# A gated mix of a state-space layer and a feed-forward layer: first loads in another order, six GELUs ahead of the sines, and part of the angle tables on GpSimd and ScalarE

## The chip, the core and the metric

The kernel runs on one core of a Trainium2 chip. The metric is the device time of one execution in microseconds; the median of 12 runs of the kernel before is 217.12 us. The core has TensorE (matmuls, into PSUM), VectorE, ScalarE, GpSimd, and SyncE, which here only issues transfers. Each engine works through its own instructions in order and waits for the others by semaphores.

## The reference

```python
x = A_x                                            # (1, 2048, 640), bfloat16
g = sigmoid((x * gate_w).sum(-1, keepdims=True))
a = S5(x)      # Bu = x @ B_bar.T ; h_t = Lam_bar * h_(t-1) + Bu_t ; a = 2 * Re(h @ C.T) + x * Dskip
b = gelu(x @ w1 + b1) @ w2 + b2                    # 640 -> 1728 -> 640
return g * a + (1 - g) * b
```

S5 has 640 complex states. `Lam_bar = exp(dt * Lambda)` has a modulus r and an angle theta per state. B_x is not used.

## The kernel before, in words

The 2048 tokens are four chunks of 512. For each chunk there are three matmul stages. `ff1(c)` computes the hidden layer of the feed-forward branch in 13 full tiles of 128 features and a last one of 64 that also holds the gate's column; each tile is five matmuls of 512 columns into one PSUM bank, and one GELU on ScalarE (`ff1_act`, L256) empties the bank into `gel`. `ssm(c)` computes x times B in ten banks, which ScalarE copies to `bu` (L537). `fin_b(c)` and `fin_a(c)` multiply by w2 and by C, and VectorE mixes both into `ot`, which SyncE stores. PSUM has eight banks (pool `ps`).

VectorE runs the recurrence. It turns `bu` by the angle (multiplications with the tables TCOS and TSIN of cosines and sines for 512 steps, L473 and L477), runs a real scan with factor r (L488), and turns the result back into `hs`. `fold(ks)` (L448 to L461) multiplies C by a complex factor: ScalarE fills two `ft` buffers (L451, L453), VectorE combines them (L457).

The tables are made at the start. From the logarithm of dt and the two parts of Lambda, three rows each of five blocks of 128 (`prmA`), a small matmul turns the rows to columns (L327), copied as `colA`. VectorE forms the angles of 128 steps for five blocks (L368 to L370), ScalarE takes sine and cosine (L377, L379) and those of 20 single angles (L385, L386); VectorE extends them to 256 steps (L406 to L411) and to 512 steps block by block (L414 to L421): two casts into the lower half of TCOS and TSIN, and for the upper half a multiplication by a column followed by a multiply-add. A second row tile, `prmB`, holds the bias b1 and the gate's weights (L389, `colB`); the GELUs need it. ScalarE keeps one set of function tables at a time: the exponential, the sine and the GELU each need a table load.

While the weights arrive, TensorE works on chunk 0 by strips. Four strips of 128 tokens are loaded (`load_xn`), turned by matmuls with the identity (`turn`), copied to `xT` by VectorE and ScalarE (`turned`, L223 and L225), and multiplied with those blocks of w1's first 768 columns (`w1a`, five blocks of 128 rows) that are there (`strip`). Six banks collect the first six feature tiles (FA = 6). Blocks 0 and 2 come by ScalarE's queue and serve the strips; blocks 1, then 4 and 3 come by SyncE's queue and serve all 512 tokens at once. Eight matmuls of ones (L213) run before the first strip is there.

TensorE, VectorE and ScalarE run in the order in which the kernel's text issues their instructions. For VectorE this order comes from a planner: `later` puts an operation with a ready time and a cost in a list, and `let_out` issues those that a clock (`ck.dve`, `ck.pe`, `ck.act`) says would have begun. `ck.dve` is set by hand to 27.0 ahead of the first scan (L422). Transfers and GpSimd's instructions are put in order by the framework's scheduler. Each transfer by SyncE's or ScalarE's queue gets one of eight counters in turn, and waits for the last transfer that used the same counter.

Of the kernel before, what the change touches and what calls it, by code (L numbers as in the profile page):

```python
# [10 lines left out]
ALU = mybir.AluOpType  # L11
ACT = mybir.ActivationFunctionType
BF16 = mybir.dt.bfloat16
# [3 lines left out]
P = 128  # L17
# [15 lines left out]
FA = 6  # L33
# [8 lines left out]
def kernel(  # L42
# [38 lines left out]
    xT = [const.tile([P, KD, CH], BF16, name=f"xT{c}") for c in range(NCH)]  # L81
    w1a = [const.tile([P, cut1], BF16, name=f"w1a_{kd}") for kd in range(KD)]
    w1b = [const.tile([P, n1b], BF16, name=f"w1b_{kd}") for kd in range(KD)]
# [31 lines left out]
    def load_xn(c, a0=0, a1=TPC, queue=None):  # L115
        if a0 == 0:
            xn[c] = xnp.tile([P, TPC, D], BF16, name="xn")
        r0 = c * CH + a0 * P
        (queue or nc.sync).dma_start(out=xn[c][:, a0:a1, :], in_=x2d[r0:r0 + (a1 - a0) * P, :].rearrange("(a p) d -> p a d", p=P))

    def load_w1a(queue, kd):
        queue.dma_start(out=w1a[kd][:], in_=B_w1[kd * P:(kd + 1) * P, 0:cut1])

    def rows(queue, dst, v):
        queue.dma_start(out=dst, in_=v.rearrange("(j p) -> j p", p=P))  # L125
# [3 lines left out]
    load_xn(0, 1, 2)  # L129
    load_w1a(nc.scalar, 2)  # L130
    load_xn(0, 2, 3)
    nc.vector.memset(prmA[:], 0.0)
    nc.vector.memset(prmB[:], 0.0)
    rows(nc.scalar, prmA[0:KS, :], A_log_dt)
    rows(nc.scalar, prmA[KS:2 * KS, :], A_Lambda_im)
    rows(nc.scalar, prmA[2 * KS:3 * KS, :], A_Lambda_re)
    load_xn(0, 3, 4)
    for kd in (1, 4, 3):
        load_w1a(nc.sync, kd)
    rows(nc.sync, prmB[KS:NB, :], B_b1[0:(KF - 1) * P])  # L140
# [17 lines left out]
    nc.sync.dma_start_transpose(out=CT_im[:], in_=A_C_im[:, :])  # L158
    nc.sync.dma_start(out=w2_sb[:, 0:KF - 1, :], in_=B_w2[0:(KF - 1) * P, :].rearrange("(kf p) d -> p kf d", p=P))
    for h in range(2):  # L160
# [4 lines left out]
    nc.sync.dma_start_transpose(out=xT[3][:], in_=x2d[3 * CH:4 * CH, :])  # L165
    load_xn(1)

    ctx.enter_context(tc.manual_schedule(engines={E.PE, E.DVE, E.Activation}))

# [38 lines left out]
    ones = lambda n: nc.const_aps.tensor(1.0, [P, n], BF16)  # L208
    warm = const.tile([P, 1], F32, name="warm")
    nc.scalar.activation(out=warm[:], in_=ones(1), func=ACT.Exp)  # L210
    pA = bank()
# [36 lines left out]
    gbs = [None] * NT  # L248
    def ff1_mm(p, c, kf, kd, t0=0, t1=CH, first=None, last=KD - 1):
        w = w1a[kd][:, kf * P:(kf + 1) * P] if kf < FA else w1b[kd][:, (kf - FA) * P:(kf - FA + 1) * P]  # L250
        nc.tensor.matmul(p[:, t0:t1], lhsT=w, rhs=xT[c][:, kd, t0:t1],  # L251
                         start=(kd == 0) if first is None else first, stop=(kd == last), skip_group_check=first is not None)
        pe(t1 - t0)
# [55 lines left out]
    def strip(kd, t0, t1, first, f0=0, f1=FA):  # L309
        for kf in range(f0, f1):  # L310
            ff1_mm(banks[kf], 0, kf, kd, t0, t1, first, 3)

    def turn_all(a):
        tB = bank()
        for i in range(3):
            turn(tB, i * P, a, i)
        turned(nc.vector, tB, 0, a, 0, 1)
        turned(nc.vector, tB, P, a, 1, 3)
        for i in range(2):
            turn(pA, i * P, a, 3 + i)  # L320
        turned(nc.scalar, pA, 0, a, 3, 5)

    strip(0, 0, P, True)
    turn_all(1)
    strip(2, 0, P, False)
    strip(0, P, HT, True)
    nc.tensor.matmul(pA[:, HT:HT + 3 * KS], lhsT=prmA[:], rhs=ident[:, 0:3 * KS], start=True, stop=True, skip_group_check=True)  # L327
    nc.vector.tensor_copy(out=colA[:], in_=pA[:, HT:HT + 3 * KS])
    nc.scalar.activation(out=dt16[:], in_=ldt_c, func=ACT.Exp)
    strip(2, P, HT, False, 0, 3)  # L330
    turn_all(2)
    nc.vector.tensor_copy(out=dt32[:], in_=dt16[:])
    nc.vector.tensor_tensor(out=dtl[:], in0=dt32[:], in1=lre_c, op=ALU.mult)
    nc.vector.tensor_tensor(out=th_c[:], in0=dt32[:], in1=lim_c, op=ALU.mult)
    nc.vector.tensor_scalar(out=thp_c[:], in0=th_c[:], scalar1=INV_2PI, scalar2=None, op0=ALU.mult)
    strip(2, P, HT, False, 3, FA)
    strip(0, HT, HT + P, True)
    turn_all(3)
    nc.scalar.activation(out=r_c[:], in_=dtl[:], func=ACT.Exp)
    strip(2, HT, HT + P, False)  # L340
    strip(0, HT + P, CH, True)
    strip(2, HT + P, CH, False)
    strip(1, 0, CH, False)

# [31 lines left out]

    nc.scalar.activation(out=FS[:, :, 0:HC], in_=red, func=ACT.Sin, scale=TWO_PI_M)  # L377
    nc.vector.scalar_tensor_tensor(out=ab, in0=red, scalar=-1.0, in1=red, op0=ALU.mult, op1=ALU.max)
    nc.scalar.activation(out=FC[:, :, 0:HC], in_=ab, func=ACT.Sin, scale=-TWO_PI_M, bias=halfpi[:])  # L379
    nc.vector.tensor_tensor(out=two[:].rearrange("p (n k) -> p n k", n=NQ), in0=thp_c[:].rearrange("p (o k) -> p o k", o=1).to_broadcast([P, NQ, KS]),  # L380
                            in1=span4[:].rearrange("p (n o) -> p n o", o=1).to_broadcast([P, NQ, KS]), op=ALU.mult)
    nc.vector.tensor_copy(out=kq[:], in_=two[:])
    nc.vector.tensor_tensor(out=redq[:], in0=two[:], in1=kq[:], op=ALU.subtract)
    nc.vector.scalar_tensor_tensor(out=absq[:], in0=redq[:], scalar=-1.0, in1=redq[:], op0=ALU.mult, op1=ALU.max)
    nc.scalar.activation(out=sq[:], in_=redq[:], func=ACT.Sin, scale=TWO_PI_M)  # L385
    nc.scalar.activation(out=cq[:], in_=absq[:], func=ACT.Sin, scale=-TWO_PI_M, bias=halfpi[:])  # L386
    for kf in range(FA):
        if kf == 3:
            nc.tensor.matmul(pA[:, 0:NB], lhsT=prmB[:], rhs=ident[:, 0:NB], start=True, stop=True, skip_group_check=True)  # L389
            nc.vector.tensor_copy(out=colB[:], in_=pA[:, 0:NB])  # L390
            for j in range(KD):
                nc.vector.tensor_copy(out=w1b[j][:, n1b - 1:n1b], in_=pA[:, j:j + 1])
        for kd in (4, 3):
            ff1_mm(banks[kf], 0, kf, kd, 0, CH, False, 3)
    for kf in range(FA):
        ff1_act(banks[kf], 0, kf)
    two_banks = [bank(), bank()]
# [16 lines left out]
    for ks in range(KS):  # L414
        nc.vector.tensor_copy(out=TCOS[:, ks, 0:HB], in_=FC[:, ks, :])
        nc.vector.tensor_copy(out=TSIN[:, ks, 0:HB], in_=FS[:, ks, :])
        for dst, X, xs, Y in ((TCOS, FS, nsH, FC), (TSIN, FC, sH, FS)):
            t = work.tile([P, HB], F32, name="g")
            nc.vector.tensor_scalar(out=t[:], in0=X[:, ks, :], scalar1=xs[:, ks:ks + 1], scalar2=None, op0=ALU.mult)
            nc.vector.scalar_tensor_tensor(out=dst[:, ks, HB:CH], in0=Y[:, ks, :],  # L420
                                           scalar=cH[:, ks:ks + 1], in1=t[:], op0=ALU.mult, op1=ALU.add)  # L421
    ck.dve = 27.0  # L422

# [256 lines left out]
    fin_a(0)  # L680
    load_xn(2)
    ssm(2, {KS - 1: lambda: first_banks(1)})
    fin_b(1, seeds(1))
    fin_a(1)
    load_xn(3)
    ssm(3)
# [38 lines left out]
```

## Time and profile before

| what | us |
|---|---|
| median of 12 runs | 217.12 (216.9 to 218.6) |
| the profiled execution's own time | 216.95 |
| its span, first to last instruction | 215.2 |
| TensorE busy | 209.4 (97%) |
| VectorE busy | 190.1 (88%) |
| ScalarE busy | 101.1 (47%) |
| GpSimd busy | 1.1, in the first 2 us |
| mean granted clock of TensorE | 0.997 |

Times inside the profile count from the span's start. A row of the timeline gives start, duration, engine, line, operation, output and input, and in brackets how long the engine stood idle before it and for whom. The start of an instruction can lie before the end of the one ahead of it, since engines overlap them; the distance of two starts is then what an instruction costs. Busy time by stage:

```profile
core 0: us, PE busy (x) PEld busy (x) DVE busy (x) ACT busy (x) POOL busy (x), PEclk, DMA share, GB/s
...
3.60:5.75 2.15, 1.85 (x16) 1.51 (x15) 0.90 (x4) 1.76 (x3) 0.00 (x0) 1.00 0.92 291
5.75:13.10 7.35, 7.29 (x73) 4.95 (x74) 6.20 (x26) 4.70 (x11) 0.00 (x0) 1.00 1.11 253
13.10:21.50 8.40, 8.35 (x57) 4.22 (x57) 8.16 (x19) 8.39 (x14) 0.00 (x0) 1.00 0.99 196
21.50:57.80 36.30, 36.14 (x186) 16.76 (x186) 35.40 (x88) 22.69 (x40) 0.00 (x0) 1.00 0.86 191
57.80:87.30 29.50, 29.18 (x196) 15.26 (x197) 28.53 (x50) 21.98 (x38) 0.00 (x0) 1.00 0.01 1
```

The columns are the stretch, its length, the busy time and number of instructions of TensorE, of its weight loads, of VectorE, ScalarE and GpSimd, then clock, share and rate of the transfers.

### The profile page before, as it was taken

How to read it: one execution, taken by the hardware profiler on the slowest of the kernel's cores; microseconds unless marked ns; L12 is line 12 of the kernel's file. 1: busy time of each engine (PE TensorE's matmuls, PEld its weight loads, DVE VectorE, ACT ScalarE, POOL GpSimd, SP SyncE). 2: the span in 40 equal slices, each digit the busy share in tenths (PEclk: the TensorE clock that was granted, in tenths of full speed). 3: DMA queues.
4: the chain of work that ended last, by engine and by line, in shares of the span. 5: the costliest groups of instructions: out<-in, count | busy, mean ns of one | idle time of the engine just before them, and what ended most of it. 6: DMA issues, size and time to landing. Idle time of an engine off the chain costs nothing.

```text
span 215.2 us, 3529 instructions
## 1 busy us (share of the span) xinstructions
PE 209.4 (97%) x1366; PEld 117.0 (54%) x1385; DVE 190.1 (88%) x396; ACT 101.1 (47%) x183; POOL 1.1 (0%) x12
## 2 busy tenths in 40 slices
PE   8999999999999999999999999999999999999993
PEld 4745444454454544775445677444455477654773
DVE  2899999999999999898999999799999999994252
ACT  2599556665866696203563210456682422204200
POOL 1000000000000000000000000000000000000000
PEclk9999999999999999999999999999999999999998
DMA  6999999994000000061000005100000000100011
GB/s 203 284 176 205 194 221 339 212 190 132 3 0 0 3 2 0 12 182 64 0 0 3 0 0 186 61 0 2 0 5 12 0 3 30 61 34 0 0 64 62
DMA packets 30324, 15.84 MB, mean 74 GB/s; under 512 B 22883, under 2 KB 30307, under 8 KB 30307
## 3 DMA queue, kind: packets, MB, share of 16 engines
q1 hardware_dynamic: 29844, 15.18, 29.0%
q10 hardware_dynamic: 462, 0.43, 0.6%
q8 instruction: 11, 0.18, 0.3%
q14 instruction: 7, 0.05, 0.1%
HBM read 7.48 MB, written 2.62 MB: 47 GB/s over the span
## 4 chain that ended last, share of the span: by engine, by line
PE 95%; DMA 1%; ACT 1%; issue 1%; DVE 0%; ACTq 0%
PE bank L592 26%; PE bank L251 26%; PE bank L651 20%; PE bank L534 20%; DMA xn<-in_A_x_dram 1%; PE bank L608 1%; PE bank L277 1%; ACT L210 1%; PE bank L216 0%; DVE ot L656 0%; ACT xT L225 0%; ACTq L125 0%; ACT warm L210 0%; PE bank L267 0%; PE bank L389 0%
## 5 line engine op out<-in xcount | busy, mean ns | idle before, releaser
L592 PE MATMUL bank<-w_sb,gel 128*128 128x128 bf16 (+1 forms) x408 | 56.9, 297 | 0.7 <-issue 0.5
L592 PEld LDWEIGHTS <-gel 128*128 128x128 bf16 x416 | 32.2, 98 | 25.5
L537 ACT ACTIVATE bu<-bank 128x512 bf16<-128x512 f32 x40 | 23.9, 597 | 38.9 <-PE bank L534 38.3
L256 ACT ACTIVATE gel<-bank,colB 128x512 bf16<-128x512 f32 x52 | 34.0, 695 | 11.9 <-PE bank L251 11.1
L651 PEld LDWEIGHTS <-hs 128*128 128x128 bf16 x330 | 31.6, 98 | 11.6
L488 DVE TENSOR_TENSOR_SCAN g<-r_c,carry,v 128x512 bf16<-128x512 f32 x30 | 37.4, 1270 | 0.0
L251 PE MATMUL bank<-xT,w1b 128*128 128x512 bf16 x137 | 30.8, 379 | 0.2
L600 ACT ACTIVATE gb<-bank,gcol 128x512 f32<-128x512 f32 (+1 forms) x32 | 15.1, 526 | 33.5 <-PE bank L608 17.3
L251 PE MATMUL bank<-xT,w1a 128*128 128x512 bf16 (+1 forms) x152 | 27.5, 332 | 0.2
L651 PE MATMUL bank<-CT_re,hs 128*128 128x320 bf16 (+2 forms) x165 | 27.1, 295 | 0.0
L651 PE MATMUL bank<-CT_im,hs 128*128 128x320 bf16 (+2 forms) x165 | 27.1, 295 | 0.0
L656 DVE SCALAR_TENSOR_TENSOR ot<-bank,gcol,gb 128x320 bf16<-128x320 f32 (+2 forms) x33 | 17.5, 532 | 10.7 <-PE bank L651 8.7
L534 PE MATMUL bank<-xT,BT_im 128*128 128x512 bf16 x99 | 24.8, 379 | 0.1
L534 PE MATMUL bank<-xT,BT_re 128*128 128x512 bf16 x97 | 24.4, 379 | 0.2
L251 PEld LDWEIGHTS <-w1b 128*128 128x128 bf16 x140 | 13.7, 98 | 16.4
L251 PEld LDWEIGHTS <-w1a 128*128 128x128 bf16 x156 | 13.6, 99 | 12.4
L567 DVE TENSOR_TENSOR bank<-xn,Dbc 128x320 f32<-128x320 bf16 (+2 forms) x33 | 14.5, 480 | 2.0 <-ACT gb L600 1.9
L534 PEld LDWEIGHTS <-BT_im 128*128 128x128 bf16 x100 | 9.8, 98 | 11.8
L469 DVE TENSOR_TENSOR v<-wa,wb 128x512 bf16<-128x512 bf16 x40 | 15.2, 421 | 0.6
L534 PEld LDWEIGHTS <-BT_re 128*128 128x128 bf16 x100 | 9.6, 98 | 11.0
L581 ACT ACTIVATE bank<-b2bc 128x512 f32<-128x512 bf16 (+1 forms) x24 | 11.7, 529 | 7.7 <-DVE ot L656 7.7
L469 DVE TENSOR_TENSOR wa<-TCOS,g 128x1024 bf16<-128x1024 bf16 x20 | 13.7, 685 | 0.1
(100 smaller groups left out, 151.5 us busy)
## 6 DMA issues: line engine op xcount, KB each, us to landing
out_dram<-ot SPq DMA_DIRECT2D x15, 160.0 KB, 1.8
w_sb<-in_B_w_dram SPq DMA_DIRECT2D x1, 2080.0 KB, 10.3
xn<-in_A_x_dram SPq DMA_DIRECT2D x3, 640.0 KB, 5.3
w1b<-in_B_w_dram SPq DMA_DIRECT2D x5, 240.0 KB, 4.3
xn<-in_A_x_dram SPq DMA_DIRECT2D x4, 160.0 KB, 3.3
w1a<-in_B_w_dram SPq DMA_DIRECT2D x3, 192.0 KB, 2.9
w1a<-in_B_w_dram ACTq DMA_DIRECT2D x2, 192.0 KB, 3.3
w2l<-in_B_w_dram SPq DMA_DIRECT2D x2, 80.0 KB
```

The lines of the kernel that those rows point to most:

```text
L251: nc.tensor.matmul(p[:, t0:t1], lhsT=w, rhs=xT[c][:, kd, t0:t1], start=(kd == 0) if first is None else first, stop=(kd == last), skip_grou ...
L256: nc.scalar.activation(out=gel[c][:, kf, :], in_=p[:, :], func=ACT.Gelu_apprx_tanh, bias=b1_c[:, kf:kf + 1])
L469: nc.vector.tensor_tensor(out=o, in0=a, in1=b, op=op)
L488: nc.vector.tensor_tensor_scan(s["g"][:, ri, :], r_c[:, ks:ks + 1].to_broadcast([P, CH]), s["v"][:, ri, :], init, ALU.mult, ALU.add)
L534: nc.tensor.matmul(p[:], lhsT=BT[ks >= KSA][:, kd, (ks % KSA if ks < KSA else ks - KSA) * P:][:, 0:P], rhs=xT[c][:, kd, :], start=(kd == 0 ...
L537: nc.scalar.activation(out=bu[:, ri, :], in_=p[:], func=ACT.Identity)
L567: dve_now(ck.pe, 0.45, lambda: nc.vector.tensor_tensor(out=p[:, 0:d1 - d0], in0=xn[c][:, a, d0:d1], in1=Dbc[:, d0:d1], op=ALU.mult))
L581: nc.scalar.activation(out=v, in_=src, func=ACT.Identity)
L592: nc.tensor.matmul(p[:, col:col + d1 - d0], lhsT=gel[c][:, kf, a * P:(a + 1) * P], rhs=w2_sb[:, kf, d0:d1], start=False, stop=False, skip_ ...
L600: nc.scalar.activation(out=gbs[ti][:, d0:d1], in_=p[:, col:col + d1 - d0], func=ACT.Identity, scale=gcol[:, 1, ti:ti + 1])
L651: nc.tensor.matmul(p[:, 0:d1 - d0], lhsT=hs[c][:, j, lo:lo + P], rhs=CT[:, j % KS, d0:d1], start=False, stop=(j == 2 * KS - 1), skip_group ...
L656: nc.vector.scalar_tensor_tensor(out=ot[:, d0:d1], in0=p[:, 0:d1 - d0], scalar=gcol[:, 0, ti:ti + 1], in1=gbs[ti][:, d0:d1], op0=ALU.mult, ...
```

## The change

- Loads: ScalarE's queue carries w1a's blocks 0 and 1, and blocks 2 and 3 in one transfer of 384 KB (`w1a23`), then loads its first table and runs the small activation that calls for it (`warm`). The three `prmA` rows go to SyncE's queue, behind the four strips; block 4 follows them.
- w2 comes in five transfers instead of one; the token rows of chunks 1 to 3 in two each.
- The strips use blocks 0 and 1; then come block 2 for all tokens, the bias matmul (`prmB`), and blocks 3 and 4. The small matmul for `prmA` moves behind all turns.
- VectorE's copy of `colB` and the five gate columns stand ahead of its work on the angles. The six GELUs of the first tiles stand ahead of the sines.
- Tables to 512 steps: for block 0 VectorE multiplies, for blocks 1 to 4 GpSimd does; the ten casts become two ScalarE copies of 1280 columns. GpSimd now also runs in the text's order from there on, and the products lie in the scratch tile `scr`. `ck.dve` is set to 26.0, and VectorE's planned order changes with it in places up to the end.

```diff
-    load_w1a(nc.scalar, 2)
+    load_w1a(nc.scalar, 1)
     load_xn(0, 2, 3)
+    nc.scalar.dma_start(out=w1a23[:], in_=B_w1[2 * P:4 * P, 0:cut1].rearrange("(k p) f -> p k f", p=P))
+    warm = const.tile([P, 1], F32, name="warm")
+    nc.scalar.activation(out=warm[:], in_=nc.const_aps.tensor(1.0, [P, 1], BF16), func=ACT.Exp)
+    load_xn(0, 3, 4)
     nc.vector.memset(prmA[:], 0.0)
     nc.vector.memset(prmB[:], 0.0)
-    rows(nc.scalar, prmA[0:KS, :], A_log_dt)
-    rows(nc.scalar, prmA[KS:2 * KS, :], A_Lambda_im)
-    rows(nc.scalar, prmA[2 * KS:3 * KS, :], A_Lambda_re)
-    load_xn(0, 3, 4)
-    for kd in (1, 4, 3):
-        load_w1a(nc.sync, kd)
+    rows(nc.sync, prmA[0:KS, :], A_log_dt)
+    rows(nc.sync, prmA[KS:2 * KS, :], A_Lambda_im)
+    rows(nc.sync, prmA[2 * KS:3 * KS, :], A_Lambda_re)
+    load_w1a(nc.sync, 4)
...
-    nc.sync.dma_start(out=w2_sb[:, 0:KF - 1, :], in_=B_w2[0:(KF - 1) * P, :].rearrange("(kf p) d -> p kf d", p=P))
+    for k0, k1 in ((0, 3), (3, 6), (6, 9), (9, 11), (11, KF - 1)):
+        nc.sync.dma_start(out=w2_sb[:, k0:k1, :], in_=B_w2[k0 * P:k1 * P, :].rearrange("(kf p) d -> p kf d", p=P))
...
-    load_xn(1)
-    ctx.enter_context(tc.manual_schedule(engines={E.PE, E.DVE, E.Activation}))
+    for a in (0, H):
+        load_xn(1, a, a + H)
+    ctx.enter_context(tc.manual_schedule(engines={E.PE, E.DVE, E.Activation, E.Pool}))
...
     strip(0, 0, P, True)
     turn_all(1)
-    strip(2, 0, P, False)
+    strip(1, 0, P, False)
     strip(0, P, HT, True)
+    strip(1, P, HT, False, 0, 3)
+    turn_all(2)
+    strip(1, P, HT, False, 3, FA)
+    strip(0, HT, HT + P, True)
+    turn_all(3)
+    strip(1, HT, HT + P, False)
     nc.tensor.matmul(pA[:, HT:HT + 3 * KS], lhsT=prmA[:], rhs=ident[:, 0:3 * KS], start=True, stop=True, skip_group_check=True)
...
     strip(0, HT + P, CH, True)
-    strip(2, HT + P, CH, False)
-    strip(1, 0, CH, False)
+    strip(1, HT + P, CH, False)
+    strip(2, 0, CH, False)
+    nc.tensor.matmul(pA[:, 0:NB], lhsT=prmB[:], rhs=ident[:, 0:NB], start=True, stop=True, skip_group_check=True)
+    nc.vector.tensor_copy(out=colB[:], in_=pA[:, 0:NB])
...
-    nc.scalar.activation(out=FS[:, :, 0:HC], in_=red, func=ACT.Sin, scale=TWO_PI_M)
...
+    for kf in range(FA):
+        for kd in (3, 4):
+            ff1_mm(banks[kf], 0, kf, kd, 0, CH, False)
+    for kf in range(FA):
+        ff1_act(banks[kf], 0, kf)
+    nc.scalar.activation(out=FS[:, :, 0:HC], in_=red, func=ACT.Sin, scale=TWO_PI_M)
+    nc.scalar.activation(out=FC[:, :, 0:HC], in_=ab, func=ACT.Sin, scale=-TWO_PI_M, bias=halfpi[:])
...
     for ks in range(KS):
-        nc.vector.tensor_copy(out=TCOS[:, ks, 0:HB], in_=FC[:, ks, :])
-        nc.vector.tensor_copy(out=TSIN[:, ks, 0:HB], in_=FS[:, ks, :])
-        for dst, X, xs, Y in ((TCOS, FS, nsH, FC), (TSIN, FC, sH, FS)):
-            t = work.tile([P, HB], F32, name="g")
-            nc.vector.tensor_scalar(out=t[:], in0=X[:, ks, :], scalar1=xs[:, ks:ks + 1], scalar2=None, op0=ALU.mult)
+        part = [scr[:, (2 * ks + i) * HB:(2 * ks + i + 1) * HB] for i in range(2)]
+        engine = nc.vector if ks == 0 else nc.gpsimd
+        for t, X, xs in ((part[0], FS, nsH), (part[1], FC, sH)):
+            engine.tensor_scalar(out=t, in0=X[:, ks, :], scalar1=xs[:, ks:ks + 1], scalar2=None, op0=ALU.mult)
+        for dst, t, Y in ((TCOS, part[0], FC), (TSIN, part[1], FS)):
             nc.vector.scalar_tensor_tensor(out=dst[:, ks, HB:CH], in0=Y[:, ks, :],
-                                           scalar=cH[:, ks:ks + 1], in1=t[:], op0=ALU.mult, op1=ALU.add)
-    ck.dve = 27.0
+                                           scalar=cH[:, ks:ks + 1], in1=t, op0=ALU.mult, op1=ALU.add)
+    nc.scalar.activation(out=TCOS[:, :, 0:HB], in_=FC, func=ACT.Identity)
+    nc.scalar.activation(out=TSIN[:, :, 0:HB], in_=FS, func=ACT.Identity)
+    ck.dve = 26.0
...
-    load_xn(2)
+    load_xn(2, 0, H)
+    load_xn(2, H, TPC)
...
```

## The prediction

> **What bounds the kernel now.** I read the chain of waits first, then the timeline of the first 30 us, then that of 55 to 90 us, and the rows of VectorE, ScalarE and GpSimd for durations.
>
> ```profile
> ## 4 chain that ended last, share of the span: by engine, by line
> PE 95%; DMA 1%; ACT 1%; issue 1%; DVE 0%; ACTq 0%
> ```
>
> TensorE is the bound: in order of time its chain runs without a break from 5.75 us to 211.8 us. What follows is VectorE's last operation and the last store, which the change leaves alone. So an edit can only gain in the first 5.75 us, and can lose wherever TensorE is made to wait later. The start, in the timeline:
>
> ```profile
> 1.15 0.29 POOL masks.py:199 TENSOR_SCALAR_AFFINE_SELECT ident<-ident 128x128 bf16<-128x128 bf16 x1
> ...
> 3.63 0.26 ACTq L125 DMA_DIRECT2D prmA<-in_A_Lambda_re_dram  x1
> ...
> 3.93 1.28 ACT L210 ACT_TABLE_LOAD   x1 [3.93 <-DMA xn<-in_A_x_dram]
> ...
> 4.33 0.80 PE L251 MATMUL bank<-xT,w1a 128*128 128x128 bf16 x6
> ...
> 5.33 0.37 ACT L225 ACTIVATE xT<-bank 128x256 bf16<-128x256 f32 x1
> ...
> 5.75 0.27 PE L216 MATMUL bank<-ident,xn 128*128 128x128 bf16 x2 [0.30 <-ACT xT L225]
> ...
> 5.86 0.83 PE L251 MATMUL bank<-xT,w1a 128*128 128x128 bf16 x12
> ```
>
> ScalarE's third parameter row waits at its queue until 3.63, the table load stands behind it, and the copy of L225 behind that; TensorE is idle from 5.24 (its third turn of the second strip starts at 5.14 and takes 0.107) to 5.75. Also seen: 128-column matmuls start 0.107 us apart before 5.2 us and 0.056 apart after 5.8. VectorE and ScalarE then make the sine tables and begin the scans at 27.76:
>
> ```profile
> 13.01 1.28 ACT L256 ACT_TABLE_LOAD   x1
> 13.03 0.83 DVE L406 TENSOR_TENSOR gel<-hs,cq 128x640 f32<-128x640 f32 x1
> ...
> 17.82 0.16 DVE L413 TENSOR_SCALAR nsH<-sq 128x5 f32<-128x5 f32 x1
> ...
> 27.76 0.69 DVE L469 TENSOR_TENSOR wa<-TCOS,bu 128x1024 bf16<-128x1024 bf16 x1
> ```
>
> From there VectorE is nearly full (28.5 of the 29.5 us from 57.8 to 87.3), and here is the place where it can reach TensorE:
>
> ```profile
> 75.96 0.89 DVE L457 SCALAR_TENSOR_TENSOR CT_re<-CT_re,c2re,ft 128x640 bf16<-128x640 bf16 x1 [0.22 <-ACT ft L453]
> ...
> 77.62 0.82 ACT L451 ACTIVATE ft<-CT_im,n2im 128x640 f32<-128x640 bf16 x1
> ...
> 79.06 1.90 ACT L256 ACTIVATE gel<-bank,colB 128x512 bf16<-128x512 f32 x3
> 81.36 0.69 ACT L256 ACTIVATE gel<-bank,colB 128x512 bf16<-128x512 f32 x1 [0.39 <-PE bank L251]
> ```
>
> The fold on ScalarE (L451) needs a buffer that VectorE's fold (L457) frees, GELUs stand behind it in ScalarE's queue, and their PSUM banks are what TensorE needs next. Today ScalarE has caught up with TensorE by 81.36.
>
> **The change, part by part.** *Start.* The three parameter rows leave ScalarE's queue, so its table load follows three issues of about 0.45 us from 0.72: about 2.1 to 3.4, done before the first strip is there (3.66). TensorE's idle 0.51 us goes. In it, at the slow spacing, it does the two turns and some 2.3 matmuls of the next strip: 4.3 x 0.056 = 0.24 us gained. Given back: the parameter matmul (L327) now comes 0.33 us (six matmuls) after the last turn and shares its bank with ScalarE's copy of that turn; the copy takes 0.38 (L225) and starts some 0.2 after it, so the matmul waits about 0.25. Net between 0 and 0.1; I take 0.05. If TensorE came to its fast spacing earlier than 5.75, as another run may, up to 0.6 more would be gained, since the old kernel waits for ScalarE until 5.7 in any case.
>
> The Trainium skill (TensorE: Matmul & The Clock Gate, Part 1) says that the clock rises after a busy window of about 3.4 us that runs freely, so the turn moves from run to run. The 0.107 and 0.056 agree with it; by this rule the gain would be spread over 0 to 0.6 instead of 0.05.
>
> *Transfers.* The rows go to SyncE in place of two w1a loads: 3 x 0.3 against 2 x 0.47, so SyncE's later issues move little. Each transfer waits for the one eight before it, so the w1b loads now begin when the 384 KB transfer lands. From 3.6 to 5.75 us 291 GB/s arrive; the strips and w1a's first four blocks are 1.4 MB from 1.7 us on, so this transfer ends near 6.5 and w1b starts 0.4 later than now (6.13); it is needed from 13.1 to 14.8, and arrived by 12.5. The last strip lands near 6.0 instead of 5.2 and is turned at 7.3 (now 7.86). w2 in five pieces and the split strips cost SyncE 4 x 0.5 us behind 30.5; next comes the xT transpose now issued at 33.97 and needed at 72.9. The later pieces are behind stores, tens of us early. All hidden: 0. Without that cover each late us would be one us.
>
> *Sines behind the first six GELUs.* The six strips' GELUs now come first, so ScalarE loads four tables. VectorE waits for the bias matmul before its angle work: bias copied at 10.6, GELU table to 12.2, six GELUs x 0.57 (7.62 for 13) to 15.6, sine table to 16.9, sines (0.74+0.74+0.3) to 18.7. VectorE's products (L406) start there, 5.7 us later than 13.03. The PSUM banks last until then: 8 tiles are held, the next comes at 21.4, when the GELU after the fourth table load (20.0) has freed one.
>
> *Angle tables.* VectorE gives up ten casts (0.20 each, start to start) and eight multiplies (0.38): from nsH on it has 2 x 0.27 + 10 x 0.40 = 4.6 us in place of 9.9. So alone it begins the scans at 23.6 + 4.6 = 28.2, against 27.76. ScalarE gets there too: seven GELUs 20.0 to 24.0, gelN and gz to 24.3, two copies of 1280 columns (estimate 1.27 each: 0.74 for 640 columns plus as many again at the slope between rows) to 26.8, two evictions to 27.9.
>
> *GpSimd.* Eight multiplies of 128x256 on GpSimd: the trace has none. Nearest rows: iota 0.235 (writes 128 columns) and the affine select 0.292 (reads and writes 128). Twice the latter for twice the columns is 0.58; below, 0.235. If they run wholly beside VectorE, the last ends at 23.6 + 8 x 0.58 = 28.2 and the scans start at 28.7: 0.5 to 0.9 us late. If no VectorE operation of this part runs beside a GpSimd operation, it is 23.6 + 4.6 + 8 x 0.58 = 32.8, 5.1 late. No row has both engines on such tiles at once; I take the middle for 0.58, 30.8, that is 3.0 late.
>
> The Trainium skill (SBUF — State Buffer, Who interferes with whom) says VectorE operations with two SBUF inputs and GpSimd operations exclude each other through a shared port pair, for a whole instruction. That speaks against the offload: by it the sum would be the late end, 32.8; without it the early end, 28.7. No row of this profile decides it.
>
> *What lateness costs.* VectorE's order was also made anew, for scans at 26.0 rather than 27.0: before the fourth fold (75.96) there now stand two more additions (0.7 us with the second), so it ends at 76.85 + 0.7 + late. ScalarE's last fold starts then, takes 1.44, and five GELUs follow (5 x 0.57 + 0.12): 82.0 + late. TensorE reaches tile 11 of that feed-forward at 72.7 + 11 x 1.08 (five matmuls of 0.216 each) = 84.6; four seed banks, the last tile's bank and its own leave two of the eight, so tile 8's GELU must be done. About 2.5 us of lateness would be absorbed; VectorE's 0.5 us of idling for ScalarE's folds grows with it, so I take 1.9. Beyond that VectorE, full to the next chunks, hands on one us for one. So 3.0 late costs 1.1 us, no cost below 1.9, 5.1 costs 3.2.
>
> **Sum.** The profiled execution took 216.95 us (span 215.2), the median is 217.12, 0.17 above, and I carry the change to the median: 217.12 - 0.05 + 1.1 = 218.2.
>
> **Rivals.** *The offload hides.* GpSimd runs beside VectorE, lateness is 0.5 to 0.9, TensorE never waits: 216.5 to 217.1, by the run's turn of the clock. For it: ScalarE's 27.9 and VectorE's 28.2 are both within 1.9 of today. Against: VectorE's idle time is some 1 us from 57.8 to 87.3. *GpSimd is the bound of the table stage* (slower still): an operation of 1.0 us, which is 3.4 times the affine select, would begin the scans at 32.1 even with full overlap: 4.3 late, 2.4 lost, 219.5. This decides from 0.7 us an operation on. Against: the rows. *The 384 KB transfer starves the strips*: with half of the 0.3 MB/us from 4.2 on, the last strips land at 5.1 and 6.0; were the transfer served first, they come at about 6.4 and 6.9, against turns at 6.4 and 7.3: at most 0.3 lost, 217.4. *The start doesn't gain*, since the parameter matmul's wait takes it all: 217.1, inside the first rival.
>
> **How the numbers follow.** Forecast (both engines hinder each other in part, 0.5 to 3.2 lost): 0.52. Offload hides: 0.32. GpSimd bound by its own: 0.11. Starved strips or a stall not seen here: 0.05. The likeliest case spans 217.5 to 220.3; the range goes down to 216.6 to hold most of the first rival. About 0.2% (0.43 us) is what a measurement here can tell from no change. Slower: 0.50 of the forecast, 0.11 and 0.03 = 0.64. The first rival divides evenly, and takes the rest: faster 0.17, same 0.19.
>
> **What would show it.** Right: table load before 3.5 us and no wait before the second turn; L406's products at 18.7; GpSimd's operations near 0.6 and stretched or VectorE's L423 stretched beside them; first scan product after 30; a wait of TensorE on ScalarE between 83 and 88 us. Wrong: scans at 28.5 or earlier and an unbroken chain from 5.3 us on; or a wait of TensorE in the first 15 us.

## The result, and the profile after

The changed kernel takes 220.17 us (219.80 to 221.23, 8 runs) against 217.08 (216.89 to 218.60, 32 runs of the kernel before beside it): a ratio of 1.0147, 95% interval 1.0132 to 1.0161. It is 3.1 us slower; 1.1 was forecast. The profiled execution took 220.08 us with a span of 218.3.

The chain that ended last, in the page of after:

```profile
## 4 chain that ended last, share of the span: by engine, by line
DVE 43%; PE 42%; ACT 5%; DMA 4%; POOL 3%; issue 1%; POOLq 1%; SPq 0%; DVEq 0%; ACTq 0%
```

TensorE held 95% of it before. Now VectorE holds as much as TensorE: the chain runs through GpSimd's multiplies (POOL 3%) and VectorE's scans until about 127 us, and TensorE waits for it. Where the time goes is seen by putting the same TensorE instruction of both profiles side by side:

| TensorE at | before | after | later by |
|---|---|---|---|
| the first w1b matmul of chunk 0 | 13.14 | 13.67 | 0.53 |
| the last long run of output matmuls, chunk 0 | 65.67 | 66.21 | 0.54 |
| the same of chunk 1 | 116.86 | 120.30 | 3.44 |
| the same of chunk 3 | 193.88 | 197.67 | 3.79 |
| end of the last matmul | 211.78 | 215.57 | 3.79 |
| end of the span | 215.17 | 218.29 | 3.12 |

So there are three pieces: 0.5 lost at the start, 2.9 and then 0.35 lost behind 66 us, and 0.67 gained behind the last matmul (the tail). The rows of after's timeline that belong to the losses, in order of time:

```profile
7.00 0.45 PE L220 MATMUL bank<-ident,xn 128*128 128x128 bf16 x5 [0.97 <-DMA xn<-in_A_x_dram]
...
19.53 0.82 DVE L409 TENSOR_TENSOR gel<-hs,cq 128x640 f32<-128x640 f32 x1 [4.03 <-ACT cq L399]
...
24.32 0.16 DVE L416 TENSOR_SCALAR nsH<-sq 128x5 f32<-128x5 f32 x1
...
25.65 1.21 POOL L421 TENSOR_SCALAR gel<-hs,sq 128x256 f32<-128x256 f32 x1
...
27.73 0.92 POOL L421 TENSOR_SCALAR gel<-hs,sq 128x256 f32<-128x256 f32 x1
...
28.63 0.92 POOL L421 TENSOR_SCALAR gel<-hs,nsH 128x256 f32<-128x256 f32 x1
28.69 0.69 DVE L423 SCALAR_TENSOR_TENSOR TSIN<-hs,cq,gel 128x256 bf16<-128x256 f32 x1 [0.21 <-POOL gel L421]
...
32.28 0.48 DVE L423 SCALAR_TENSOR_TENSOR TSIN<-hs,cq,gel 128x256 bf16<-128x256 f32 x1 [0.20 <-POOL gel L421]
32.68 0.68 DVE L474 TENSOR_TENSOR wa<-TCOS,bu 128x1024 bf16<-128x1024 bf16 x1
...
82.31 0.88 DVE L462 SCALAR_TENSOR_TENSOR CT_re<-CT_re,c2re,ft 128x640 bf16<-128x640 bf16 x1
...
83.22 0.83 ACT L456 ACTIVATE ft<-CT_im,n2im 128x640 f32<-128x640 bf16 x1 [2.17 <-DVE CT_re L462]
...
84.81 4.13 ACT L260 ACTIVATE gel<-bank,colB 128x512 bf16<-128x512 f32 x7
85.53 1.24 PE L255 MATMUL bank<-xT,w1b 128*128 128x512 bf16 x4 [1.52 <-ACT gel L260]
...
87.84 2.32 PE L255 MATMUL bank<-xT,w1b 128*128 128x512 bf16 x10 [1.07 <-ACT gel L260]
...
127.50 0.84 PE L656 MATMUL bank<-CT_re,hs 128*128 128x320 bf16 x5 [0.19 <-DVE bank L572]
```

Read from the bottom: at 127.50 TensorE waits 0.19 us for VectorE's seeds (x times Dskip, which VectorE writes into an output bank before the matmuls with C add to it); that is the part of the 0.35 that a row shows. Before that it waits twice, 1.52 and 1.07 us, for ScalarE's GELUs. Those stand behind the last fold on ScalarE, which waited 2.17 us for VectorE's fold product of the fourth block; that comes at 82.31, at 75.96 before. VectorE began its scans at 32.68 (before 27.76), because each multiply-add waits for a GpSimd multiply, and these come 0.90 apart. From `nsH`, which ends the common part of the table work, to the first scan product it is 8.36 us. The products of the sines began at 19.53 (before 13.03). At 7.00 TensorE waits 0.97 us for the third strip.

### The profile page after: what moved, and what is told of

It reads as the page before. It is cut to its first block, busy times and chain, and to the rows that moved or that the text cites. A ratio compares the mean times of both kernels' runs of the same rounds, so it can differ in the third digit from the quotient of the medians.

```text
span 218.3 us, 3530 instructions
## 1 busy us (share of the span) xinstructions
PE 209.3 (96%) x1366; PEld 116.5 (53%) x1385; DVE 187.7 (86%) x378; ACT 103.3 (47%) x186; POOL 8.6 (4%) x20
## 4 chain that ended last, share of the span: by engine, by line
DVE 43%; PE 42%; ACT 5%; DMA 4%; POOL 3%; issue 1%; POOLq 1%; SPq 0%; DVEq 0%; ACTq 0%
PE bank L656 15%; PE bank L597 13%; DVE g L493 12%; PE bank L255 7%; DVE wb L474 6%; DVE wa L474 6%; PE bank L539 5%; DVE v L474 4%; DVE hs L474 3%; POOL gel L421 3%; DMA xn<-in_A_x_dram 2%; DVE CT_re L462 2%; DMA out_dram<-ot 2%; DVE bank L572 2%; ACT gel L260 2%; DVE CT_im L462 1%
## 5 line engine op out<-in xcount | busy, mean ns | idle before, releaser
L542 ACT ACTIVATE bu<-bank 128x512 bf16<-128x512 f32 x40 | 23.1, 615 | 35.6 <-PE bank L539 35.6
L260 ACT ACTIVATE gel<-bank,colB 128x512 bf16<-128x512 f32 x52 | 33.5, 690 | 9.7 <-PE bank L255 9.6
```

The costliest lines, as they stand in the source:

```text
L260: nc.scalar.activation(out=gel[c][:, kf, :], in_=p[:, :], func=ACT.Gelu_apprx_tanh, bias=b1_c[:, kf:kf + 1])
L542: nc.scalar.activation(out=bu[:, ri, :], in_=p[:], func=ACT.Identity)
```

## The experiments

Each changes the kernel named, and each computes the whole reference. Diffs are cut to their core.

### What lateness costs

**The planner told the truth.** The changed kernel with one number:

```diff
-    ck.dve = 26.0
+    ck.dve = 32.6
```

> The changed kernel with one number altered: the planner that writes VectorE's order is told that the scans can begin at 32.6 us (ck.dve = 32.6) instead of 26.0; every operation stays. Theory (lateness costs only because the order made for 26.0 puts scan work that cannot be done in time ahead of the folds that ScalarE's GELUs wait for): first scan product still at 32.7, but the fold products stand earlier in VectorE's order, TensorE's waits between 83 and 88 us fall to under 0.5 us, time 217.3 to 218.0, since only the start (0.5) is left. Rival (VectorE is full from there on, so lateness is handed on one for one whatever the order): the loss moves to a later place, time 219.8 to 220.5.

Measured: 216.78 us, ratio to before 0.9982 (0.9972 to 0.9992). Its timeline:

```profile
32.57 0.68 DVE L476 TENSOR_TENSOR wa<-TCOS,bu 128x1024 bf16<-128x1024 bf16 x1
...
61.98 0.88 DVE L464 SCALAR_TENSOR_TENSOR CT_re<-CT_re,c2re,ft 128x640 bf16<-128x640 bf16 x1 [0.48 <-ACT ft L460]
...
76.64 0.88 DVE L464 SCALAR_TENSOR_TENSOR CT_re<-CT_re,c2re,ft 128x640 bf16<-128x640 bf16 x1
...
78.05 0.82 ACT L458 ACTIVATE ft<-CT_im,n2im 128x640 f32<-128x640 bf16 x1
...
81.78 0.69 ACT L260 ACTIVATE gel<-bank,colB 128x512 bf16<-128x512 f32 x1 [0.39 <-PE bank L255]
```

The scans begin as late as in the changed kernel, and yet the first fold product comes at 61.98 instead of 68.53, ScalarE's last fold waits for nobody, and ScalarE is idle for TensorE by 81.78, as before. TensorE waits for no other engine after 7 us. 3.4 us come from one number that no engine computes with: TensorE, ScalarE and GpSimd run the same order as in the changed kernel, VectorE alone another. Theory held, and the rival's later loss is nowhere: lateness as such costs nothing. The time is 0.5 below the theory's range, which left out the 0.6 that the changed kernel gains at the tail.

**The planner's old number.** The changed kernel with `ck.dve = 27.0`:

> The changed kernel with the planner's number put back from 26.0 to the 27.0 of the kernel before; every operation stays. First scan product at 32.7 as in the changed kernel. Theory (the loss grows with the distance between the planner's number and the true start, and the one from 27.0 to 26.0 moves two additions ahead of a fold): waits of TensorE at 84 to 88 us of about 2.4 instead of 2.6, later ones of 0.3, time 218.5 to 219.5, clearly under the changed kernel's 220.2. Rival (only lateness counts, the number hardly): 219.9 to 220.4.

Measured: 219.31 us, 1.0120 (1.0102 to 1.0139): inside the range, but the waits lie elsewhere than expected. At 86.02 there are 0.84 us, and 1.75 come later, 0.25 of them at 125.74:

```profile
86.02 2.32 PE L255 MATMUL bank<-xT,w1b 128*128 128x512 bf16 x10 [0.84 <-ACT gel L260]
...
178.17 0.84 PE L658 MATMUL bank<-CT_re,hs 128*128 128x320 bf16 x5 [1.00 <-DVE bank L574]
...
181.55 0.84 PE L658 MATMUL bank<-CT_re,hs 128*128 128x320 bf16 x5 [0.50 <-DVE bank L574]
```

At the later places TensorE waits for VectorE's seeds of the output banks: the same lateness, let out at another place of the order. In this profile TensorE loses 3.2 us behind 66 us, as much as in the changed kernel. The profiled execution took 220.15 us, though, and three of the five runs took 219.25 to 219.31; what they saved no profile shows, so the step from 26.0 to 27.0 decides nothing between theory and rival.

**The reverse.** The kernel before, nothing late, but the planner told 21.1 instead of 27.0:

> The kernel before with one number altered: the planner is told that the scans can begin at 21.1 us instead of 27.0; they still begin at 27.8, so nothing is late, but number and truth are 6.7 us apart, as in the changed kernel. Theory (what costs is the distance between the planner's number and the truth): a wait of TensorE on ScalarE of 0.8 to 2.5 us between 83 and 88 us, time 217.9 to 219.6. Rival (what costs is the late start itself): no wait, 217.1.

Measured: 219.01 us, 1.0086 (1.0072 to 1.0100).

```profile
27.82 0.69 DVE L469 TENSOR_TENSOR wa<-TCOS,bu 128x1024 bf16<-128x1024 bf16 x1
...
80.38 0.88 DVE L457 SCALAR_TENSOR_TENSOR CT_re<-CT_re,c2re,ft 128x640 bf16<-128x640 bf16 x1
...
81.29 0.83 ACT L451 ACTIVATE ft<-CT_im,n2im 128x640 f32<-128x640 bf16 x1 [2.02 <-DVE CT_re L457]
...
85.91 2.32 PE L251 MATMUL bank<-xT,w1b 128*128 128x512 bf16 x10 [0.59 <-ACT gel L256]
```

The scans are on time and the same wait appears, through the same fold. Of the 1.7 us by which TensorE's end is later in this profile, 0.9 come behind 66 us; 0.8 stand ahead of 20 us, where a w1b block came late (TensorE resumes at 14.89), which the edit does not explain. So what the order costs by this profile is 0.9, and the time falls into the theory's range with the help of the other 0.8.

**The sines first again.** The changed kernel with the four sine operations ahead of the six GELUs and the bias matmul in its old place:

```diff
+    nc.scalar.activation(out=FS[:, :, 0:HC], in_=red, func=ACT.Sin, scale=TWO_PI_M)
...
     for kf in range(FA):
+        if kf == 3:
+            nc.tensor.matmul(pA[:, 0:NB], lhsT=prmB[:], rhs=ident[:, 0:NB], ...)
...
         ff1_act(banks[kf], 0, kf)
-    nc.scalar.activation(out=FS[:, :, 0:HC], in_=red, func=ACT.Sin, scale=TWO_PI_M)
```

> The changed kernel with the sines ahead of the six GELUs again and the bias matmul back in its old place; loads, strips, GpSimd multiplies and ScalarE copies as changed. Theory (the six GELUs ahead of the sines make the lateness): products start near 13.5, first scan product at 26 to 27.5, no wait of TensorE on ScalarE between 83 and 88 us; what is left is the start (about 0.5) and a wait of the first w1b matmuls for the bias column (0 to 0.7): 217.5 to 218.3. Rival (GpSimd's multiplies are what costs, wherever they stand): the wait between 83 and 88 us stays over 1.5 us, time over 219.3.

Measured: 217.67 us, 1.0028 (1.0018 to 1.0039). Products at 14.40, first scan product at 27.56, no wait between 83 and 88 us. What is left is at the start:

```profile
14.40 0.39 PE L255 MATMUL bank<-xT,w1b 128*128 128x512 bf16 x1 [0.63 <-DVE w1b L396]
```

The order is the one made for 26.0, as in the changed kernel; with scans at 27.56 it does no harm. So neither that order nor the lateness costs by itself; the two have to disagree. The kernels in one table ("told" is the planner's number, "distance" how far it lies from the first scan product; the fifth column counts VectorE's operations between the first scan product and the first fold product):

| kernel | told | first scan product | distance | operations ahead of the first fold | fourth fold product | us |
|---|---|---|---|---|---|---|
| before | 27.0 | 27.76 | 0.8 | 78 | 75.96 | 217.08 |
| changed, told 32.6 | 32.6 | 32.57 | 0.0 | 66 | 76.64 | 216.78 |
| changed, sines first | 26.0 | 27.56 | 1.6 | 81 | 77.34 | 217.67 |
| changed, VectorE multiplies | 26.0 | 30.88 | 4.9 | 81 | 80.50 | 218.93 |
| changed, told 27.0 | 27.0 | 32.56 | 5.6 | 78 | 80.48 | 219.31 |
| before, told 21.1 | 21.1 | 27.82 | 6.7 | 86 | 80.38 | 219.01 |
| changed | 26.0 | 32.68 | 6.7 | 81 | 82.31 | 220.17 |
| changed, tables on VectorE | 26.0 | 33.77 | 7.8 | 81 | 83.40 | 222.85 |

Behind 66 us TensorE loses nothing in the profiles of the second and third row, and 1.85, 3.2, 0.9, 3.25 and 6.0 us in those of the last five (3.3 of the 6.0 at half a clock, see the next run). The distance says whether there is a loss, not how much: 6.7 us cost 0.9 in one kernel and 3.25 in another. The waits for a GELU go with the fourth fold product: at 77.3 or earlier there is none, near 80.4 one of 0.6 to 1.1 us, from 82.3 on 2.6 or more. Two kernels below fit: with the old loads the product comes at 81.78 and TensorE waits 2.6 us, with GpSimd alone at 77.55 and it does not wait.

### What the table work costs where

**All of it on VectorE again.** The changed kernel with the tables made as in the kernel before:

```diff
-        engine = nc.vector if ks == 0 else nc.gpsimd
...
+        nc.vector.tensor_copy(out=TCOS[:, ks, 0:HB], in_=FC[:, ks, :])
+        nc.vector.tensor_copy(out=TSIN[:, ks, 0:HB], in_=FS[:, ks, :])
...
-    nc.scalar.activation(out=TCOS[:, :, 0:HB], in_=FC, func=ACT.Identity)
-    nc.scalar.activation(out=TSIN[:, :, 0:HB], in_=FS, func=ACT.Identity)
```

> The changed kernel with the table work given back to VectorE (ten casts and all ten multiplies, as in the kernel before; GpSimd and ScalarE do none of it). Theory (what counts is when the first scan product starts; from 32.68 us on each us later costs TensorE one us between 83 and 88 us): VectorE needs 9.8 us from nsH (24.3) on, so the first scan product starts at 34.3, 1.6 us later than in the changed kernel, and the time is about 221.8 (221.3 to 222.2). Rival (GpSimd's operations hinder VectorE so much that the offload is worth nothing or less): first scan product at 32.7 or earlier, time 220.2 or less.

Measured: 222.85 us, 1.0268 (1.0238 to 1.0299), first scan product at 33.77. From `nsH` on that is 9.93 us against 8.36 in the changed kernel: the whole offload saves 1.6 us of the stage, as the theory had it. The time is above its range, and the profile shows why: two rows of TensorE, then its stretches (begin and end, length, TensorE's busy time and matmuls, granted clock, share and rate of the transfers).

```profile
86.62 0.59 PE L255 MATMUL bank<-xT,w1b 128*128 128x512 bf16 x1 [2.72 <-ACT gel L260]
87.43 5.72 PE L255 MATMUL bank<-xT,w1b 128*128 128x512 bf16 x13 [0.22 <-issue]
```

```profile
80.00:84.00 4.00, 3.90 (x19) 1.00 0.00 0
84.00:86.00 2.00, 0.00 (x0) 0.99 0.01 4
86.00:87.00 1.00, 0.38 (x1) 0.50 0.00 0
87.00:90.00 3.00, 2.76 (x7) 0.50 0.00 0
90.00:92.00 2.00, 2.00 (x6) 0.50 0.00 0
92.00:93.00 1.00, 1.00 (x5) 0.60 0.00 0
93.00:94.00 1.00, 1.00 (x24) 1.00 0.00 0
```

TensorE waited 2.72 us for ScalarE, its clock fell to half at 86.0 and stayed there until 92.8. The 14 matmuls behind the wait took 6.36 us (86.62 to 92.98) in place of 14 x 0.216 = 3.0: a stall of 2.7 us cost 6.0. All six runs had a mean clock of 0.985 or 0.992.

**Only GpSimd's part to VectorE.** The changed kernel with `engine = nc.vector` for all five blocks; ScalarE keeps its copies:

> The changed kernel with GpSimd's eight multiplies given to VectorE; ScalarE keeps its two copies, the planner's number stays 26.0. Theory (on GpSimd and VectorE together each of these pairs costs 0.90 us, on VectorE alone 0.27 + 0.40 = 0.67): from nsH (24.3) VectorE needs 10 x 0.27 + 10 x 0.40 = 6.7, so the first scan product starts at 31.2, 1.5 us earlier than in the changed kernel, and the waits at 84 to 88 us fall from 2.6 to about 1.1: time 218.4 to 218.9. Rival (the offload to GpSimd is worth something and only the ScalarE copies are not): first scan product at 32.7 or later, time 220.2 or more.

Measured: 218.93 us, 1.0081 (1.0069 to 1.0093), first scan product at 30.88. On VectorE alone a pair costs 0.66:

```profile
29.16 0.48 DVE L425 SCALAR_TENSOR_TENSOR TSIN<-hs,cq,gel 128x256 bf16<-128x256 f32 x1
29.56 0.35 DVE L423 TENSOR_SCALAR gel<-hs,nsH 128x256 f32<-128x256 f32 x1
29.82 0.35 DVE L423 TENSOR_SCALAR gel<-hs,sq 128x256 f32<-128x256 f32 x1
30.08 0.48 DVE L425 SCALAR_TENSOR_TENSOR TCOS<-hs,cq,gel 128x256 bf16<-128x256 f32 x1
```

The multiplies stand 0.26 apart and take 0.35 each; on GpSimd they stand 0.90 apart. From `nsH` to the first scan product this kernel needs 6.80 us, the changed one 8.36: handing multiplies to an idle engine made the stage 1.6 us longer, and ScalarE's copies alone shorten it by 9.93 - 6.80 = 3.1. The wait at 86 us falls to 1.07, about as expected; the time lies at the upper end of the theory's range.

**GpSimd alone.** The kernel told 32.6, with VectorE's multiply-adds of blocks 1 to 4 held back until GpSimd is done:

```diff
+    for ks in (0, 4, 3, 2, 1):
         for dst, t, Y in (...):
             nc.vector.scalar_tensor_tensor(out=dst[:, ks, HB:CH], ...)
```

> The kernel that is told 32.6, with VectorE's eight multiply-adds for ks 1 to 4 held back until GpSimd's last multiply (they begin with ks = 4), so that from about 26 us on GpSimd works alone. Theory A (GpSimd and VectorE take turns: 0.90 is one GpSimd operation and one multiply-add of 0.40): GpSimd's operations start 0.5 to 0.6 us apart once VectorE rests, the last ends near 29.5, first scan product at 32.5 to 33. Theory B (0.90 is GpSimd's own time and VectorE only waits for it): they stay 0.9 apart, the last ends near 32, first scan product at 35.0 to 35.5. Time 216.6 to 217.2 in A; in B up to 218.

Measured in one run: 216.05 us. Theory B held:

```profile
24.86 1.02 POOL L423 TENSOR_SCALAR gel<-hs,sq 128x256 f32<-128x256 f32 x1
25.86 0.92 POOL L423 TENSOR_SCALAR gel<-hs,nsH 128x256 f32<-128x256 f32 x1
...
30.36 0.92 POOL L423 TENSOR_SCALAR gel<-hs,sq 128x256 f32<-128x256 f32 x1
```

VectorE rests from 25.7 to 31.3, and GpSimd still takes 0.92 an operation, 0.90 apart. That is its own pace, and the 0.90 of the changed kernel is not VectorE's doing; only the second operation there, 1.21 us against 1.02 here, may be. The first scan product came at 34.48, 0.5 ahead of B's range since this run's `nsH` was 0.8 us earlier than in the changed kernel. It is the latest of all kernels, and TensorE still never waited for ScalarE.

**Without GpSimd.** The fastest kernel below, with VectorE's multiplies and the number at 31.0:

> The fastest kernel so far (told late, 384 KB transfer behind the fourth strip) with GpSimd's multiplies on VectorE and the planner's number at 31.0. Theory (TensorE has no wait left that the table work reaches): first scan product near 29.8, time unchanged at 215.9 to 216.3. Rival (the offload relieves VectorE enough to count later): 216.5 or more, with waits of TensorE after 80 us.

Measured: 216.38 us, 0.9967 (0.9956 to 0.9979), between the theory's range and the rival's. The first scan product comes at 30.98, 1.2 later than expected, and TensorE has no wait after 80 us, so the rival's mark is missing: in these two kernels, both told nearly the truth, the table work does not reach the end. Between their two profiles the first w1b matmul differs by 1.07 us (12.46 and 13.53, see below) and the end of the last matmul by 1.06, so behind the start they are alike.

### The start

**The old loads.** The changed kernel with the loads, strips and parameter matmul of the kernel before:

> The changed kernel with the loads, the strips' order and the parameter matmul of the kernel before; GELUs ahead of the sines and the table work as changed. Theory (0.5 us of the loss is the start, where the third strip comes late beside the 384 KB transfer; 2.6 to 2.9 come at 84 to 88 and at 127 us): no wait over 0.3 us for a strip, first w1b matmul near 13.1, the waits at 84 to 88 us stay near 2.6; time 219.4 to 219.9. Rival A (the start is the whole cause, and the later waits only follow from it): waits at 84 to 88 us under 1 us, time under 218. Rival B (the start costs nothing): 220.2.

Measured: 220.90 us, 1.0154 (1.0134 to 1.0175): above the theory's range. The start behaves as expected (third strip turned at 6.72 without a wait for it, first w1b matmul at 13.14), and so do the two waits. But:

```profile
85.01 1.24 PE L253 MATMUL bank<-xT,w1b 128*128 128x512 bf16 x4 [1.53 <-ACT gel L258]
87.32 4.00 PE L253 MATMUL bank<-xT,w1b 128*128 128x512 bf16 x10 [1.07 <-ACT gel L258]
```

Ten matmuls take 4.00 us; in the changed kernel's profile, behind the same two waits, they take 2.32. The clock fell again (mean 0.992 over the span), which costs 1.7 and hides what the start gave back. The runs divide by it: the three at 0.992 took 220.90 to 221.06 us, the two at 1.000 took 219.61 and 220.19, against the theory's 219.4 to 219.9. What the old loads are worth in time stays open.

**The 384 KB transfer behind the strips.** The kernel told 32.6, with `w1a23` on SyncE's queue:

```diff
-    nc.scalar.dma_start(out=w1a23[:], in_=B_w1[2 * P:4 * P, 0:cut1]...)
...
     load_xn(0, 3, 4)
+    nc.sync.dma_start(out=w1a23[:], in_=B_w1[2 * P:4 * P, 0:cut1]...)
```

> The kernel that is told 32.6, with the 384 KB transfer of w1a's blocks 2 and 3 moved from ScalarE's queue to SyncE's, behind the fourth strip. Theory (beside that transfer the strips on SyncE's queue get too little): TensorE's wait for the third strip falls from 0.8 us to under 0.2, the first w1b matmul starts at 12.8 to 13.1 instead of 13.56, time 216.1 to 216.4. Rival (the strips come as late without it, since all transfers share the bandwidth): wait of 0.6 or more, or one of the same size for w1a's block 2 later on, time 216.7 to 216.9.

Measured: 216.09 us, 0.9961 (0.9948 to 0.9974), the fastest of those run more than once.

```profile
4.59 0.45 PE L220 MATMUL bank<-ident,xn 128*128 128x128 bf16 x5
...
5.81 0.44 PE L220 MATMUL bank<-ident,xn 128*128 128x128 bf16 x5
...
6.95 0.44 PE L220 MATMUL bank<-ident,xn 128*128 128x128 bf16 x5
```

The third strip is turned at 5.81, no wait, and the first w1b matmul starts at 12.46, 0.3 ahead of the range. Bytes by queue in the traces, in KB for each half microsecond from 4.0 us on:

```
                               4.0  4.5  5.0  5.5  6.0  6.5
changed   SyncE's (strips)     108   18   24  115  140   57
          ScalarE's (w1a23)     48   98  129   65   49   25
moved     SyncE's (all)        160  176  180  178  174   62
```

In the changed kernel the strips' queue nearly stops between 4.5 and 5.5 us, while the other carries its 384 KB. All seven profiles with that transfer on ScalarE's queue show it (6 to 38 KB in each of these half microseconds), none of the other seven does (59 KB or more). What this costs depends on when TensorE's clock rises: in the changed kernel it rose at 3.48 us (wait of 0.97, w1b at 13.67), in the kernel told 27.0 at 6.56 (no wait, 13.53), with the transfer moved at 3.37 (no wait, 12.46), and in the kernel without GpSimd, moved too, at 6.72 (no wait, 13.53). In these four an early clock is worth 1.1 us with the strips on time and nothing without them. The third strip itself does not come equally late in each execution: with the same loads it is turned at 6.52 in the profile of "all of it on VectorE" (first w1b matmul at 13.18) and at 6.18 in that of "GpSimd alone" (12.88). Over the seven profiles with the changed loads that matmul starts at 12.88 to 13.67, over the five with the old ones at 13.14 to 13.33, so the 0.53 of the changed kernel's profile is the most that was seen, not a fixed cost.

### The tail

**The pieces alone.** The kernel before with w2 in five pieces and the token rows in halves:

> The kernel before with one part of the change alone: w2 in five pieces and the token rows in halves, six transfers more. In the profile of before the span ends 3.4 us after TensorE's last matmul, in that of the changed kernel and of the four runs so far 2.7 to 2.8 us. Theory A (the tail hangs on something that moved with the number of transfers): TensorE's end unchanged at 211.8, tail 2.8 us, time 216.4 to 216.7. Theory B (the tail of before's one profile is an accident, or hangs on another part; the pieces are hidden as forecast): 216.9 to 217.3.

Measured: 216.55 us, 0.9983 (0.9971 to 0.9995). TensorE ends at 211.95, the span at 214.82, 2.87 later (before 3.39). So the 0.5 to 0.7 us that the tail is shorter belong to this part of the change.

**Two transfers more.** The kernel before with w2 in three pieces:

```diff
-    nc.sync.dma_start(out=w2_sb[:, 0:KF - 1, :], ...)
+    for k0, k1 in ((0, 5), (5, 10), (10, KF - 1)):
+        nc.sync.dma_start(out=w2_sb[:, k0:k1, :], ...)
```

> The kernel before with w2 in three pieces: two transfers more on SyncE's queue and nothing else. In before SyncE stands still for 0.46 us behind its 79th recorded instruction, which is one of its closing waits; in the kernel with the pieces alone the same pause comes behind its 79th too, at 207.4 us, where a store's wait hides it. Theory A (the pause sits at a fixed place of SyncE's instruction stream; two more instructions put the long closing wait behind it): pause again behind the 79th, hidden, tail 2.8 us, time 216.4 to 216.7. Theory B (the pause goes with the last transfers, or with six more): 216.9 to 217.3.

Measured: 217.23 us, 1.0007 (0.9998 to 1.0016). The pause again stands behind SyncE's 79th recorded instruction, but it is not hidden:

| kernel | pause behind the 79th | what SyncE does there | tail |
|---|---|---|---|
| before | 213.80 to 214.26 | closing waits, behind the long one | 3.39 |
| pieces alone | 207.44 to 207.92 | between two stores | 2.87 |
| two more | 213.96 to 214.42 | closing waits, behind the long one | 3.5 |
| moved (above) | 203.88 to 204.35 | between two stores | 2.7 |

The place of the pause is fixed, as theory A said. What I missed is that two more transfers also change which of the closing waits is the long one: it became the first of them, so the pause still followed it, and the time is the one that theory B gave, though not for its reason. What SyncE does in the pause no row shows. The pause of 0.46 accounts for most of the 0.52 between the first two tails.

## Why the prediction was right or wrong

**Direction and path: right.** Late scans, a late fold, GELUs behind it, TensorE waiting between 83 and 88 us: the rows of after are those that the last paragraph of the prediction named. One of its signs of being wrong came too, a wait of TensorE in the first 15 us. Sizes and one reason were wrong. The start was missed by 0.58 to one side and the tail by 0.67 to the other; that they nearly cancel is luck. What is left is the term "3.0 late costs 1.1 us": it was 4.9 late and cost 3.25.

**"Start ... I take 0.05" gained: wrong, 0.53 lost in this profile.** The table load came at 2.13 as forecast and the wait for ScalarE's copy went. The step that failed is "all hidden: 0" for the 384 KB transfer, with "at most 0.3 lost" as the rival. That step reckoned with half of the bandwidth for each queue; the bytes by queue show 18 and 24 KB against 98 and 129. The transfer itself landed at 7.99, not at 6.5, and the w1b loads began at 8.00, 1.9 later than before instead of 0.4; for them TensorE did not wait. The "up to 0.6" for an early clock was right as a size: with the transfer moved the first w1b matmul starts 0.68 earlier than before. The Trainium skill (DMA: Bandwidth & Descriptors, Queues, rings and completion order) says that each DMA engine takes turns between its queues packet by packet; the half microseconds at 4.5 and 5.0 us do not look like equal turns, and the measurement decides.

**"Products start there, 5.7 us later": nearly right.** 6.5 later; of the 0.8 more, 0.53 is the start.

**GpSimd's "0.58" and "I take the middle": wrong, and this sized the lateness.** This is the step that failed for the main loss: the price of an operation was taken from rows of other operations. From the third on (the first two took 1.00 and 1.21) an operation takes 0.92, 0.90 apart, with or without VectorE beside it, so eight of them alone end the stage at 32.68, 4.9 late instead of 3.0. Of the 1.9 more, 0.7 was there at `nsH` (24.32 instead of 23.6) and 1.2 is GpSimd's pace. The prediction called 0.7 us the point from which GpSimd decides, and gave that rival 0.11; its mechanism is the one that came. The Trainium skill (GPSIMD Engine Reference, 4.1 Engine selection) says that one-input operations on GpSimd run at about line rate; here 0.90 stands against VectorE's 0.26, 3.4 times as much. The rule that the prediction took from it (SBUF — State Buffer, Who interferes with whom), a lock for a whole instruction, led to 32.8 and so close to the measured start, but not for its reason: beside GpSimd six of VectorE's multiply-adds take 0.69 instead of 0.48, GpSimd's 0.92 does not change, and 0.90 for a pair is less than the 0.92 + 0.48 of two operations that exclude each other.

**"VectorE ... hands on one us for one": the size right, the reason wrong.** With 4.9 late, 1.9 absorbed and the rest handed on, the formula gives 3.0; 2.9 and 0.35 came. Here the step "VectorE, full to the next chunks" failed: started as late and told the truth, the kernel loses nothing behind 66 us. The order written for 26.0 puts 81 operations ahead of the first fold, the one for 32.6 puts 66, and the scan work that stands behind the folds there makes TensorE wait nowhere later. The prediction saw the two additions that the new number moved, and did not ask what the order itself was worth.

**"Which the change leaves alone": wrong, 0.6 gained at the tail.** The pieces were costed at nothing, and nothing waits for them; but with six more transfers SyncE's pause no longer falls among its closing waits.

Sum in the profile: 0.53 + 2.9 + 0.35 - 0.67 = 3.1, against -0.05 + 1.1.

## What to carry to other kernels

Where an order is written out by a planner, an estimate in it is part of the program: after each change that moves a start, put the measured start into it, and cost a change by when the operation that others wait for comes out in that order. Price work on another engine by a row of that engine before handing it over, since an idle engine can be slower than the busy one's own time. A load on a second queue is not free for the first: what is needed first goes ahead of it, on one queue.

## What was not expected of the hardware

**A stall can cost its length twice.** In two of the profiles the clock fell to half behind TensorE's waits, for 6.83 us (after 2.72 us of waiting) and for 3.41 (after 1.53 and 1.07), and the matmuls behind took 3.3 and 1.7 us longer. In the changed kernel's profile the same two waits left it at 1.00. The time between two changes of the clock is a multiple of 3.413 us in every profile. Counted in such steps from the clock's rise, the changed kernel's two waits fall into two steps, with 1.4 and 1.2 us idle; in the two halved cases one step holds 2.0 or 2.1. In all thirteen profiles with a record of the clock, a step with up to 1.8 us idle left it at 1.00 and one with 2.0 or more was followed by half; no run tests such a limit on purpose. The Trainium skill (TensorE: Matmul & The Clock Gate, Part 1) has the clock fall after an idle window of about 3.4 us. The lengths, two windows and one, agree; the idle time does not, since in the 3.41 us ahead of the fall TensorE was idle for only 2.1 us (83.90 to 85.98) in one case and 2.0 (0.96 and 1.07) in the other, and the measurement decides.

**SyncE pauses for 0.46 to 0.47 us behind its 79th recorded instruction**, in seven of the fourteen profiles; in the other seven the next one is a store that waits 2.32 us there, and a pause would not be seen. Whether it counts depends on what SyncE is doing then.
